# mLSTM with a mixture of experts: gate values computed two steps earlier, list products a position later, VectorE's order within a step changed, six weight loads at later steps

## The chip, the core and the metric

The kernel runs on one core of one Trainium2 chip. The metric is the device time of one execution in microseconds (us); a lower time is better. TensorE (PE) does the matrix products, VectorE (DVE), ScalarE (ACT) and GpSimd (POOL) the elementwise work, SyncE (SP) issues nearly all transfers. Each engine takes its instructions strictly in the order in which the program issues them.

## What is computed

Two parts follow each other: an mLSTM over 4 batches, 8 heads, 768 time steps and head size 40, and a mixture of 8 experts in which each of the 3,072 tokens goes to its best expert alone.

```python
for t in range(S):                                   # mLSTM, state C and n per batch and head
    m_new = max(f_gate[t] + m, i_gate[t])
    f_stab, i_stab = exp(f_gate[t] + m - m_new), exp(i_gate[t] - m_new)
    C = f_stab * C + i_stab * outer(v[t], k[t]);  n = f_stab * n + i_stab * k[t];  m = m_new
    y[t] = sigmoid(o_gate[t]) * (C @ q[t]) / max(|n . q[t]|, 1)
x = y as rows (3072, 320)
logits = normed(x) @ normed(expert_emb).T / tau
e = argmax(logits);  gate = softmax(logits)[e]
out = gate * relu(x @ w1[e]) @ w2[e]
```

## The kernel before, in words

The sequence is cut into 6 chunks of 128 time steps. Chunk times batch gives 24 steps (`NS`), and the loop `for n in range(NS)` (line 1199) writes out the order of every engine's work by hand; there is no planner. Step n handles chunk n // 4 of batch n % 4. The chunk is worked on in two halves of 64.

In one step of the loop, as the program issues it before the change: SP gets the loads of step n+5 (`load_dims`, `load_rows`) and the o-gates of step n+3 (`stage_sig`); PE does `stage_add(n, 0)` (the first half's outer products, added to a state that stays in PSUM, `pcv(n)`); ACT copies that state to `c_mid` (`stage_mid`); VectorE does `stage_next` (line 630) for an earlier step: it writes half of the decayed state to `c_st`, decays the state in PSUM, and ACT later copies the other half (line 1273). PE then does `stage_scores(n + 1)` into the one PSUM tile `s`; POOL does `stage_uv(n + 2)` (values times gate); VectorE does `stage_den(n - 1)` and `stage_x(n - 1)` (the division), POOL `stage_gate(n - 1)`; VectorE does `stage_weigh(n + 1)`, which masks the scores from `s` into `w_s`; PE transposes x of step n-2 (`stage_xt`), does `stage_y(n)`, `stage_add(n, 1)` and the router's logits of step n-3 (`stage_logits`).

Between these steps stands the making of the routing lists: for a group of tokens (`GROUPS`: steps 0 to 5, 6 to 12, 13 to 23) small VectorE operations find the expert (`route_a`), the rank (`route_b`), a one-hot matrix for each step (`route_o`, line 894, into `op`) and an index factor (`route_c`, into `oa`), and PE forms products of them (`route_rank`, `route_ids`, line 899). Which step does what is the table `ROUTE` (line 951). Operations wait in the list `vq`; each `tick()` issues one of them to VectorE, and ticks stand in between the operations of a step. `route(n, 0)` empties `vq` and issues the step's products after `stage_y(n)`; `route(n, 1)` fills `vq` for the next step.

Before the loop the gates of chunk 0 are computed (`gates_scan(0)` and what follows it, lines 1053 to 1075). Those of chunks 1 to 5 go through a chain that crosses four engines: `gates_scan(1)`, `gates_chain` (a scan over the chunks, step 0), `gates_floor` (step 1), `gates_exp` (ACT, step 2), `gates_turn` (products on PE, copies `u_t` and `e_t`, `g_t`, end of step 2), and `stage_uv(4)`, the first to use them. The embeddings of the experts are normed and transposed by `embeddings(0..2)`, at steps 1, 2, 2. Chunks after the first need the gates.

Weight loads of the first two experts (`w_loads`) are issued by SP at the end of the steps that `W_AT` names; at the steps in `W1_AT` ACT and POOL split a loaded piece into two parts. After the loop come the experts: first the two largest with the tokens gathered by `gather_a` (POOL, line 311, at step 21), then the others; this part is left as it is but for `route_o`.

## Time and profile before

| what | value |
|---|---|
| median of 3 runs | 331.6 us (329.17 to 333.5) |
| the profiled execution | 328.59 us |
| its span, first to last instruction | 326.8 us, 1.8 us lie around it |
| mean granted TensorE clock | 0.973 |
| busy: PE, DVE, ACT, POOL | 93%, 69%, 49%, 52% of the span |
| loop, first `stage_y` of step 0 to that of step 23 | 11.66 to 114.20 us |

The table's last line is read from the timeline of PE. Busy shares are means over the loop and the experts, which have different limits; what the change touches lies in the first 115 us. A step is measured here from the first product of its `stage_y` to that of the next.

### The profile page before, as it was taken

The numbers are of one execution on the slowest core, as the hardware profiler recorded it, in microseconds if no ns is written. First come the engines' busy times: TensorE is split into PE (matmuls) and PEld (weight loads), VectorE is DVE, ScalarE is ACT, GpSimd is POOL, SyncE is SP. The second block draws the span as 40 slices with busy tenths as digits, with TensorE's granted clock in tenths as the row PEclk, the third lists the DMA queues.
The fourth block names the chain that finished last, engine by engine and source line by source line (L and its number), as shares of the span: only waits on it lengthen the run. The fifth ranks groups of instructions, "written<-read, shape, count | busy, mean of one in ns | idle before, by whom it ended". The sixth has DMA issues, their size and how long they took to land.

```text
span 326.8 us, 9615 instructions
## 1 busy us (share of the span) xinstructions
PE 302.7 (93%) x3637; PEld 285.8 (87%) x3637; DVE 224.3 (69%) x638; ACT 161.8 (49%) x410; POOL 168.3 (52%) x204
## 2 busy tenths in 40 slices
PE   7877998989997899999969979999999999999992
PEld 3867897978986699989969969999999999999992
DVE  6775777798999479983644786757657586695620
ACT  6394554655564466452332745437427458075310
POOL 8765584757886849350563760650560550832112
PEclk9595999999999799999999999999999999999999
DMA  5896688899999654030277978958837939656001
GB/s 154 301 308 197 185 244 270 254 273 276 256 293 262 225 146 123 3 73 22 70 251 215 304 238 158 301 196 219 262 96 207 321 128 304 196 141 194 20 21 38
DMA packets 48089, 63.31 MB, mean 194 GB/s; under 512 B 21146, under 2 KB 37990, under 8 KB 48034
## 3 DMA queue, kind: packets, MB, share of 16 engines
q1 hardware_dynamic: 45218, 54.16, 56.4%
q0 software_dynamic: 2560, 8.35, 8.4%
q8 instruction: 31, 0.51, 0.7%
q14 instruction: 24, 0.20, 0.2%
q10 hardware_dynamic: 256, 0.10, 0.1%
HBM read 47.51 MB, written 11.93 MB: 182 GB/s over the span
## 4 chain that ended last, share of the span: by engine, by line
PE 76%; DVE 10%; DMA 5%; issue 3%; ACT 3%; POOL 1%; POOLq 0%; SPq 0%; DVEq 0%
PE ph L376 28%; PE po L408 17%; PE s L573 5%; PE po_b L408 4%; PE y L654 4%; PE po_a L408 3%; PE c L612 3%; PE po L393 3%; DMA kv_s<-in_kv 3%; PE y L665 3%; PE pm L731 2%; DMA sig<-in_og 2%; DVE op L896 1%; PE px L717 1%; DVE w_s L582 1%
## 5 line engine op out<-in xcount | busy, mean ns | idle before, releaser
L427 POOL DMA_INDIRECT out<-ob,ids x20 | 22.9, 1145 | 79.2 <-DVE ob L424 70.6
L378 ACT ACTIVATE hh<-ph 128x448 fp32r<-128x448 f32 (+2 forms) x48 | 23.6, 491 | 50.7 <-PE ph L376 36.6
L408 PE MATMUL po<-w2h,hl 128*128 128x320 f32 x128 | 39.6, 309 | 0.0
L408 PE MATMUL po<-w2h,hh 128*128 128x320 f32 x128 | 39.5, 309 | 0.0
L408 PE MATMUL po<-w2l,hh 128*128 128x320 f32 x128 | 39.5, 309 | 0.0
L558 POOL TENSOR_TENSOR uv<-kv_s,u_t 64x328 f32<-64x328 f32 x47 | 34.8, 740 | 8.9 <-PE c L612 4.5
L376 PE MATMUL ph<-xh,w1h 128*128 128x448 f32 (+2 forms) x96 | 32.2, 338 | 1.7 <-DVE hh L383 1.7
L381 DVE SCALAR_TENSOR_TENSOR hl<-ph,hh 128x384 fp32r<-128x384 f32 (+1 forms) x48 | 24.4, 509 | 12.5 <-ACT hh L378 11.7
L376 PE MATMUL ph<-xh,w1l 128*128 128x448 f32 (+2 forms) x96 | 32.0, 336 | 0.0
L573 PE MATMUL s<-kq_s 128*64 128x64 f32 x768 | 29.6, 232 | 1.8 <-DVE w_s L582 1.2
L573 PEld LDWEIGHTS s<-kq_s 128*64 128x64 f32 x768 | 27.4, 146 | 2.9 <-DVE w_s L582 2.2
L197 ACT CAST w1h<-raw 128x512 fp32r<-128x512 f32 x48 | 28.9, 612 | 0.0
L200 DVE TENSOR_TENSOR w2l<-raw,w2h 128x320 fp32r<-128x320 f32 x58 | 28.1, 531 | 0.6
L424 DVE TENSOR_SCALAR ob<-po,gt 128x320 f32<-128x320 f32 x16 | 8.8, 551 | 28.0 <-PE po L408 20.1
L701 POOL TENSOR_TENSOR x<-x,sig 128x320 f32<-128x320 f32 x21 | 18.2, 866 | 17.6 <-DVE x L697 6.9
L612 PE MATMUL c<-uv,kv_s 128*40 128x82 f32 x352 | 24.1, 250 | 2.6 <-issue 1.5
L197 ACT CAST w2h<-raw 128x320 fp32r<-128x320 f32 x62 | 24.4, 457 | 3.2 <-DMA raw<-in_w 2.9
L654 PE MATMUL y<-uv,w_s 128*64 128x82 f32 x384 | 25.7, 250 | 0.0
L628 ACT COPY c_mid<-c 40x164 f32<-40x164 f32 x48 | 14.0, 292 | 23.2 <-PE c L612 22.7
L299 POOL DMA_INDIRECT xs<-x_d,ids x20 | 21.9, 1095 | 6.2 <-issue 5.8
L200 DVE TENSOR_TENSOR w1l<-raw,w1h 128x512 fp32r<-128x512 f32 x36 | 25.1, 706 | 0.0
L376 PE MATMUL ph<-xl,w1h 128*128 128x448 f32 (+2 forms) x96 | 24.5, 336 | 0.0
(314 smaller groups left out, 927.9 us busy)
## 6 DMA issues: line engine op xcount, KB each, us to landing
raw<-in_w SPq DMA_DIRECT2D x32, 320.0 KB
kv_s<-in_kv SPq DMA_DIRECT2D x24, 324.0 KB
kq_s<-in_kq SPq DMA_DIRECT2D x48, 160.0 KB
raw<-in_w SPq DMA_DIRECT2D x14, 512.0 KB
raw<-in_w SPq DMA_DIRECT2D x18, 256.0 KB
sig<-in_og SPq DMA_DIRECT2D x24, 160.0 KB
x_d<-x SPq DMA_DIRECT2D x24, 160.0 KB
x_d<-halves SPq DMA_DIRECT2D x4, 576.0 KB
```

The lines of the kernel that those rows point to most:

```text
L197: A.copy(h, src)
L200: (eng or V).tensor_tensor(lo, src, h.bitcast(F32), ALU.subtract)
L299: G.indirect_dma_start(out=xs[0 : c.shape[0], a], out_offset=None, in_=x_d[0:rows], in_offset=bass.IndirectOffsetOnAxis(ap=c, axis=0), bou ...
L376: T.matmul(ph, lt, rh, start=i == 0, stop=i == len(ops) - 1)
L378: A.activation(hh, ph, AF.Relu)
L381: V.scalar_tensor_tensor(hl[:, 0:m], ph[:, 0:m], 0.0, hh[:, 0:m].bitcast(F32), ALU.max, ALU.subtract)
L408: T.matmul(po[0 : ts_.stop - ts_.start, 0:DM], lt[f][:, ts_], rh[:, f], start=k == 0, stop=k == len(ops) - 1)
L427: store = G.indirect_dma_start(out=out, out_offset=bass.IndirectOffsetOnAxis(ap=slots, axis=0), in_=ob, in_offset=None, bounds_check=NT - ...
L558: eng.tensor_tensor(uv[n % NB][rows, :, :, r], list(rows_of(n))[1][rows], u_t[rows, j, b].unsqueeze(3).broadcast_to([L, 2, NP, D1]), ALU.mult,
L573: T.matmul(s[r * L : r * L + L, c, p], k_of(n, odd)[:, a, cs], q_of(n)[:, a, cs], start=True, stop=True,)
L612: T.matmul(pc[odd * L : odd * L + D, 2 * g : 2 * g + 2], k_rows[:, c, p], uv[n % NB][:, c, p], start=False, stop=g == 1, skip_group_check= ...
L654: T.matmul(yh[c][:, g, :, odd], w_s[n % NB][:, c, 2 * g + odd], uv[n % NB][:, c, 2 * g + odd], start=g + odd == 0, stop=n < B and c == 0, ...
```

## The change

Start: `gates_scan(1)` moves ahead of the first values (it stood after the first `stage_weigh`); `gates_chain` is cut in two (`gates_ends`, `gates_chain`) and both move from step 0 to before the loop; `gates_floor` goes from step 1 to 0; the exponentials from step 2 to 1; a new `gates_spread` (the matrix `gr`, formerly the end of `gates_exp`) stands at step 1; `gates_turn` stays in step 2 but moves ahead of `stage_y(2)`. `c_st` is cleared before the loop, the number tables are made at steps 3 and 5, the embeddings at steps 2, 3, 4, and the two sigmoids and the two warm activations of steps 0 to 2 are put in another order.

Loop: `stage_next` becomes one VectorE operation and stands after `stage_weigh(n + 1)`; both copies to `c_st` go to ACT (`stage_keep`), one step later. `stage_den`, `stage_x`, `stage_weigh`, `stage_next` now follow each other with no ticks between; then come, at one place, the rest of `vq`, the step's products, the new list and nine ticks. The product so stands ahead of `stage_xt` and `stage_y`. `ROUTE` is adapted, `route_o` makes two steps' matrices with one `tensor_tensor` in place of one with each `tensor_scalar`. `W_AT` moves loads to later steps.

```diff
-W_AT = (9, 9, 10, 12, 13, 15, 16, 17, 18, 19, 20, 22)
+W_AT = (9, 10, 12, 14, 16, 18, 19, 20, 21, 22, 22, 23)
-EMB_AT = (1, 2, 2)
+EMB_AT = (2, 3, 4)
...
                 g = g_t[:, j + 1, b].unsqueeze(2).broadcast_to([P, NP, D1])
-                (rows0, dst0, src0), (rows1, dst1, src1) = state_rows(n, c_st[b])
-                V.tensor_tensor(dst1, src1, g[rows1], ALU.mult)
-                tick()
                 V.tensor_tensor(pcv(n), pcv(n), g, ALU.mult)
-                st[n]["next"] = dst0, src0
-                tick()
+
+        def stage_keep(n):
+            if n < NS - B:
+                for rows, dst, src in state_rows(n, c_st[n % B]):
+                    A.copy(dst, src)
...
-            V.tensor_scalar(op, iota_b, grp[g]["lo"][:, b : b + 1], None, ALU.is_equal)
+            V.tensor_tensor(
+                op, iota_b.unsqueeze(1).broadcast_to([P, k, P]), bc(grp[g]["lo"][:, b : b + k], P), ALU.is_equal
+            )
...
-            12: ([], [(place_first,)]),
-            13: ([], [(place_sum,), (route_c, 0)]),
+            12: ([], [(place_first,), (place_sum,)]),
+            13: ([], [(route_c, 0)]),
             14: ([lambda: route_ids(0)], [(route_d, 0)]),
-            15: ([], [(route_a, 1)]),
-            16: ([lambda: route_rank(1)], [(route_b, 1), (gates_early[0],)]),
-            17: ([], [(route_sum, 1), (route_os, 1, 0, 3)]),
-            18: ([early_count], [(route_os, 1, 3, 6), (early_base,), (gates_early[1],)]),
-            19: ([], [(route_os, 1, 6), (route_c, 1)]),
+            16: ([], [(route_a, 1), (gates_early[0],)]),
+            17: ([lambda: route_rank(1)], [(route_b, 1), (route_sum, 1)]),
+            18: ([early_count], [(route_os, 1), (early_base,)]),
+            19: ([], [(gates_early[1],), (route_c, 1)]),
             20: ([lambda: route_ids(1)], [(route_d, 1), (early_ids,)]),
...
         V.tensor_copy(u_t[:, 0]...)
+        gates_scan(1)
         stage_uv(0, (V, G))
         V.tensor_copy(e_t[:, 0]...)
+        for t in c_st:
+            G.memset(t, 0.0)
         stage_uv(1)
-        stage_weigh(0)
-        gates_scan(1)
...
+        gates_ends()
+        stage_weigh(0)
+        gates_chain()
         for n in range(NS):
...
             stage_mid(n)
+            for k in of(n - 1, 1, NEXT_AT):
+                stage_keep(k)
             if n == 1:
-                A.activation(maxc.bitcast(F32), half, AF.Exp)
+                gates_exp()
+                A.activation(maxc.bitcast(F32), half, AF.Sigmoid)
             if n == 2:
-                gates_exp()
-            for k in of(n, 1, NEXT_AT):
-                stage_next(k)
+                stage_sigmoid(1)
             if not last:
                 stage_scores(n + 1)
...
             if n:
-                (stage_den(n - 1, 0..2), stage_x, stage_gate with ticks between)
+                (the same without ticks)
             if not last:
                 stage_weigh(n + 1)
-                tick(2)
+            for k in of(n, 1, NEXT_AT):
+                stage_next(k)
+            route(n)
+            tick(9)
             if n == 0:
-                gates_chain()
-                for t in c_st:
-                    G.memset(t, 0.0)
+                gates_floor()
             if n == 1:
-                gates_floor()
-                numbers()
+                gates_spread()
             if n == 2:
-                more_numbers()
+                gates_turn()
+                stage_uv(n + 2)
+            if n == EMB_AT[2]:
+                embeddings(2)
...
             stage_y(n)
             if n < NS - B:
                 stage_add(n, 1)
-            if n == 2:
-                gates_turn()
-                stage_uv(n + 2)
-            for k in of(n, 0):
-                stage_sigmoid(k)
-            (ACT copies of half of c_st)
+            if n != 1:
+                stage_sigmoid(n)
+            if n == 0:
+                A.activation(maxc.bitcast(F32), half, AF.Exp)
...
-            if not last:
-                route(n, 0)
-            for k in of(n, 3):
+            for k in of(n, 3, (EMB_AT[2],)):
                 stage_logits(k)
-            route(n, 1)
```

## Rows read from the trace of the kernel before

**Rows 1.** Stretches: length; PE, PEld, DVE, ACT, POOL busy us; PEclk, DMA share, GB/s
```profile
11.66:42.44 30.78, 27.07 (x535) 24.73 (x532) 21.73 (x75) 17.68 (x49) 19.81 (x39) 0.83 0.76 246
...
19.48:29.87 10.39, 7.07 (x106) 5.92 (x106) 7.45 (x28) 6.85 (x20) 6.80 (x15) 0.79 0.89 291
29.87:34.67 4.80, 4.80 (x88) 4.56 (x87) 1.30 (x4) 2.07 (x7) 1.62 (x3) 0.73 0.34 97
34.67:38.27 3.60, 3.60 (x96) 3.36 (x95) 2.26 (x8) 2.25 (x8) 2.16 (x3) 1.00 0.67 207
42.44:62.46 20.02, 18.98 (x485) 17.33 (x484) 15.40 (x64) 10.35 (x35) 13.91 (x19) 1.00 0.84 250
62.46:82.82 20.36, 18.88 (x483) 17.21 (x482) 17.19 (x53) 11.88 (x38) 13.92 (x17) 1.00 0.94 282
82.82:107.58 24.76, 22.93 (x571) 20.70 (x570) 23.11 (x76) 14.37 (x46) 19.09 (x23) 1.00 0.96 270
107.58:114.20 6.62, 5.25 (x62) 4.21 (x61) 2.19 (x7) 2.74 (x9) 5.55 (x6) 0.75 0.67 208
```

**Rows 2.** Waits of PE up to 116 us: us in total, times, longest
```profile
PE pen L1188 <- DVE en L1182: 2.5, 1, 2.5
PE pm L903 <- DVE oa L879: 1.8, 2, 1.6
PE c L612 <- issue: 1.5, 2, 1.0
PE s L573 <- DVE w_s L582: 1.2, 2, 0.7
```

**Rows 3.** Chain that ended last, 18 to 28 us: start, us, what
```profile
20.27 1.28 ACT L1116
22.11 0.76 PE pg L1135 x16
25.62 0.54 DVE en L1182
```

**Rows 4.** Timeline of VectorE, start of the kernel: start, us, what, idle before
```profile
8.24 0.49 DVE L558 TENSOR_TENSOR uv<-kv_s,u_t 64x328 f32<-64x328 f32 x1 [1.32 <-DMA kv_s<-in_kv]
9.36 0.41 DVE L1042 TENSOR_TENSOR_SCAN gs<-gf,onef 96x128 f32<-96x128 f32 x1
...
10.12 0.42 DVE L1044 TENSOR_TENSOR_SCAN gp<-gi 96x128 f32<-96x128 f32 x1
...
13.54 1.50 DVE L1091 TENSOR_TENSOR mj<-mm 32x2 f32<-32x2 f32 x3
...
19.41 0.60 DVE L1113 TENSOR_SCALAR gp<-gp,na,cl 96x128 f32<-96x128 f32 x2
```

**Rows 5.** Timeline of ScalarE and of GpSimd, start of the kernel
```profile
15.28 0.60 ACT L628 COPY c_mid<-c 40x164 f32<-40x164 f32 x2 [3.76 <-PE c L612]
...
10.69 1.52 POOL L558 TENSOR_TENSOR uv<-kv_s,u_t 64x328 f32<-64x328 f32 x2 [1.36 <-DMA kv_s<-in_kv]
...
15.08 1.30 POOL L1250 MEMSET c_st<- 128x328 f32 x4
```

**Rows 6.** VectorE's groups, 42.5 to 104.2 us: busy, mean ns, idle before
```profile
L582 DVE TENSOR_TENSOR w_s<-s,late 128x512 f32<-128x512 f32 x15 | 10.2, 681 | 0.0
L697 DVE TENSOR_TENSOR x<-y,den 128x320 f32<-128x320 f32 x15 | 7.4, 491 | 0.7
L636 DVE TENSOR_TENSOR c_st<-c,g_t 40x164 f32<-40x164 f32 x14 | 4.6, 332 | 6.9 <-PE c L612 6.7
```

**Rows 7.** All of the one-hot operations by line: duration ns min/median/max, first and last start
```profile
L896 DVE TENSOR_SCALAR op<-iota_b,lo x24: 242/249/1251, 65.9 to 139.5; 128x128 f16<-128x128 bf16 x24
```

**Rows 8.** Timeline of VectorE and PE around step 20
```profile
95.87 0.68 DVE L582 TENSOR_TENSOR w_s<-s,late 128x512 f32<-128x512 f32 x1
...
101.47 0.33 PE L903 MATMUL pm<-oa,op 128*128 128x32 f16 x7 [1.61 <-DVE oa L879]
```

**Rows 9.** GpSimd's largest group, 42.44 to 104.27 us: busy, mean ns
```profile
L558 POOL TENSOR_TENSOR uv<-kv_s,u_t 64x328 f32<-64x328 f32 x31 | 22.8, 734 | 3.0 <-PE c L612 1.8
```

More of the change, by code (lines that the diff above doesn't have):

```diff
@@ L719, in stage_xt @@
             T.transpose(px[:, 2 * P : 3 * P], x[:, DM - P : DM], ident)
[L720 removed]
+            xt = st[n]["xt"] = tp.tile([P, 3, P], F32, name=f"xt_{n}", tag="xt", bufs=3)
             A.copy(xt.rearrange("p c t -> p (c t)"), px[:, 0 : 3 * P])
@@ L892, in route_sum, with route_o @@
             yield
-        def route_o(g, b):
-            op = sm(g, f"op{b}", [P, P], F16)
-            V.tensor_scalar(op, iota_b, grp[g]["lo"][:, b : b + 1], None, ALU.is_equal)
+        def route_o(g, b, k):
+            op = sm(g, f"op{b}", [P, k, P], F16)
+            grp[g].update({f"op{b + i}": op[:, i] for i in range(k)})
+            V.tensor_tensor(
+                op, iota_b.unsqueeze(1).broadcast_to([P, k, P]), bc(grp[g]["lo"][:, b : b + k], P), ALU.is_equal
+            )
             yield
@@ L911, in route_os @@
         def route_os(g, b0=0, b1=None):
-            for b in range(b0, b1 or nt(g)):
-                yield from route_o(g, b)
+            b1 = b1 or nt(g)
+            for b in range(b0, b1, 2):
+                yield from route_o(g, b, min(2, b1 - b))
         def cntv(g):
@@ L978, in tick, with route @@
                         vq.pop(0)
-        def route(n, i):
-            if i == 0:
-                while vq:
-                    tick()
-                for f in ROUTE.get(n, [[]] * 2)[0]:
-                    f()
-            else:
-                vq.extend(f(*a) for f, *a in ROUTE.get(n, [[]] * 2)[1])
+        def route(n):
+            while vq:
+                tick()
+            products, lists = ROUTE.get(n, ([], []))
+            for f in products:
+                f()
+            vq.extend(f(*a) for f, *a in lists)
         warm = pX.tile([P, 512], F32, name="warm", tag="px")
@@ L1227, in tile_mlstm_moe @@
                 gates_early[2]()
-            if n == NS - 3:
-                while vq:
-                    tick()
             if n:
-                stage_den(n - 1, 0)
-                tick()
-                stage_den(n - 1, 1)
-                tick()
-                stage_den(n - 1, 2)
+                for k in range(3):
+                    stage_den(n - 1, k)
                 stage_x(n - 1)
@@ L1265, in tile_mlstm_moe @@
                 stage_add(n, 1)
-            if n == 2:
-                gates_turn()
-                stage_uv(n + 2)
-            for k in of(n, 0):
-                stage_sigmoid(k)
-            for k in of(n, 1, NEXT_AT):
-                if "next" in st[k]:
-                    A.copy(*st[k]["next"])
+            if n != 1:
+                stage_sigmoid(n)
+            if n == 0:
+                A.activation(maxc.bitcast(F32), half, AF.Exp)
             for k in of(n, 1):
@@ L1277, in tile_mlstm_moe @@
                 stage_sq(k)
-            for k in range(3):
-                if EMB_AT[k] == n:
-                    embeddings(k)
-            if not last:
-                route(n, 0)
-            for k in of(n, 3):
+            if n in EMB_AT[:2]:
+                embeddings(EMB_AT.index(n))
+            if n == 3:
+                numbers()
+            if n in (5, 6):
+                G.memset(xs_a[:, n - 5], 0.0)
+            if n == 5:
+                more_numbers()
+            for k in of(n, 3, (EMB_AT[2],)):
                 stage_logits(k)
-            route(n, 1)
             for _ in range(W_AT.count(n)):
```

23 lines of the change are left out of this document (12 added, 11 removed).

## The prediction

> **What bounds the kernel now.** I read the busy time by stretches first, cut at the first product of each `stage_y`, then PE's waits, then the chain in the stretch that is longest, and last the timelines of the engines that the chain names. The plain step 4 takes 3.60 us with PE busy for all of it at the full clock, VectorE for 2.26 and GpSimd for 2.16 [rows 1]. So PE's own work sets the step, and whatever a step takes over 3.60 is what a change of order can win. The sums over the loop: steps 0 to 5 take 30.78 us where six plain steps take 21.6; steps 6 to 10 take 20.02 against 18.0; steps 11 to 15 20.36 against 18.0; steps 16 to 21 24.76 against about 21.0 (21.6 less two times 0.3, since steps 20 and 21 have no `stage_add(n, 1)`; an estimate: eight of some 96 products); step 22 6.62, with two extra turns of gathered rows and PE's clock at 0.75 [rows 1]. PE's waits name the causes: 2.5 us for the embeddings' norm, 1.8 for `oa`, 1.2 for the masked scores, 1.5 for nothing that the profile shows [rows 2].
>
> Most of the surplus is step 2, with 10.39 us, and step 3, with 4.80 us at a mean clock of 0.73, that is in part at 1.2 GHz, since PE had idled before it [rows 1]. The chain there is the gate chain that the change moves: the exponentials begin with a table load of 1.28 us on ScalarE at 20.27, the turn on PE starts at 22.11, then VectorE scales the embeddings at 25.62, and only behind their transposes PE takes up step 3 [rows 3].
>
> **The start, part by part.** `gates_scan(1)` is three operations from 9.36 to 10.54, 1.2 us. Ahead of `stage_uv(0)` VectorE idles 1.32 us for a transfer [rows 4]; the scan fills that, cost nothing; without that cover it would put the first values back by 1.2. The clearing of `c_st`, 1.30 us on GpSimd, goes into its wait of 1.36 us ahead of `stage_uv(1)` [rows 5], cost nothing, at worst 1.3. The rest of `gates_chain` starts behind the first mask, some 2.5 us earlier than now; its three small copies to `mj` took 1.50 us [rows 4], next to a GpSimd operation, and will meet another one, `stage_uv(1)`. `gates_floor` now ends at 20.01 [rows 4]; one step earlier, with the chain earlier too, I put it at 15.5. Behind it on VectorE stand den, x and the mask of step 2, late by some 0.4 us, which PE does not see: the mask is wanted only by the next scores. On ScalarE the exp table is now loaded in an idle stretch of 3.76 us before 15.28 [rows 5], so that the exponentials follow `stage_mid(1)` at 15.9 and end at about 17; the table for the sigmoid follows them, 1.28 us, and `stage_mid(2)` is through at about 19.1. PE has the turn to do right after `stage_scores(3)`, some half us ahead of the 19.48 at which step 2 begins now, and nothing that it needs is late by then. It costs PE what it costs now, 1.5 us (22.11 to where the chain leaves PE), but it is now in the way of `stage_y(2)`, where formerly PE idled behind it. Behind the turn ScalarE copies `u_t`, and GpSimd does `stage_uv(4)` until about 22.5; PE wants it two steps on, at about 26. The embeddings' three transposes, about 0.4 us, come at step 4 when the norm of step 3 is long done. So step 2 becomes 3.6 + 1.5, step 3 has no idle before it and runs at the full clock, and in step 5 nothing waits for the copies of `c_st`, which now come a step later and well before `stage_y(n + 4)`.
>
> Steps 0 to 5 then: 21.6, plus 0.65 for step 0 at the half clock as now (an estimate: its excess is unchanged), 1.5 for the turn, 0.4 for the transposes: 24.1 instead of 30.78 [rows 1]. **Gain 6.7 us.** Bounds: 3.5, if the chain is late by a whole step after all; 7.5, if the turn is hidden in part.
>
> SP issues the same loads in nearly the same order (o-gates of step 1 one load earlier, the embeddings one earlier); each queue keeps its work. The number tables move to steps 3 and 5 of GpSimd, which is busy for 2.16 of 3.60 us [rows 1], so 1.4 a step are free for them.
>
> **The lists.** VectorE loses one operation of 332 ns in each of 14 steps [rows 6], 4.6 us over the loop; ScalarE gets a second copy of about that length and was busy 2.25 of 3.60 us [rows 1], so that costs nothing. VectorE's fixed work in a step becomes 2.26 - 0.33 = 1.9 us, and 1.7 are left for lists. Its idle ahead of line 636, 6.7 us for `stage_add` of PE [rows 6], goes, as den and x need only `stage_y`. The mask now stands ahead of the list work; so what is queued behind a long list is den and x of the next step and then its mask, and PE meets it only if the list runs over by more than about 1.7 us (an estimate: 3.60, less the 1.2 that the 32 scores take as a third of a step's 96 products, less the mask's 0.68).
>
> Steps 11 to 15 have 17.19 us of VectorE's work in 20.36; five of the removed operations take 1.6 out [rows 1, 6], and lists of up to 2.5 us follow plain ones, so the surplus should go but for the product of `route_ids(0)`, 0.3. **Gain 2.0 us** (0.8 to 2.2). Steps 6 to 10: 2.02 us of surplus, of which 1.04 is a single wait of PE for nothing shown [rows 2] that I can't tie to any of it, and 0.4 products that stay: gain 0.2 (0 to 1.3).
>
> Steps 16 to 21 are the hard part. VectorE is busy 23.11 of 24.76 us [rows 1]. Removed are four times 0.33. The one-hot operations of group 1 fall from seven to four, but each does 256 columns where one took 242 ns undisturbed for 128 [rows 7]; no row shows the new form, and between 0.24 and 0.48 for two I take 0.4, so this is even. And `route_ids(1)` moves forward on PE, ahead of `stage_y(20)`, while its last input stays in the list of step 19: now it comes 4.9 us after the mask of 95.87 (which ended at 96.55), and PE waited 1.61 for it at the end of a step [rows 8]. In the new order that list has nine operations in one piece, about 4 us; the mask's 0.68, the decay's 0.33 and the list add to about 5.0 from the end of the scores, and PE is back at the product after 3.6: a wait of 1.4 if VectorE is on time, up to 3.4 if it runs two us late. I take 2.3. So surplus 3.76 falls to 0.6 of products and 2.3: **gain 0.8 us** (-0.6 to 2.3).
>
> **The weight loads.** The queue's share is 0.94 to 0.96 through steps 11 to 21 and 0.67 in step 22 [rows 1], so a later load finds room, and the pieces of the first matrix still come two or three steps after their load. The second matrix and the second expert's are split only behind the loop, and the last of them is issued where now the last but one is. No gain, no loss; if one is late, the split of it blocks ScalarE and with it the relu of the experts. Step 22 keeps its 6.62 us: GpSimd's gathers and PE's unexplained waits there are not touched (0 to 2.5 gain). After the loop only the one-hot operations of group 2 change, eleven to six: 0 (-0.5 to 0.5).
>
> **Sum.** 6.7 + 0.2 + 2.0 + 0.8 = 9.7 us off the profiled execution's 328.6: 318.9. The median of the runs lies 3.0 above that execution, outside its 1.8 us around the span, and the runs scatter by 4.3; taken from the median the sum gives 321.9. I put the time between, **320.5 us**.
>
> **A rule that speaks against it.** A list operation of 242 ns took up to 1,251 [rows 7], and `mj` 1.50 us for three tiny ones [rows 4]. The Trainium skill, SBUF — State Buffer, Who interferes with whom, says that a VectorE operation with two SBUF inputs, or in a two-port mode, and a GpSimd operation that reads SBUF shut each other out for their whole length, while one that reads PSUM goes by its own port. By that rule den, x and the mask don't wait but the lists do, and lists in one piece wait at every operation of GpSimd; the trace agrees in that the mask's mean is 681 ns and x's 491 without such outliers [rows 6]. What it would make of the time is rival four.
>
> **Rivals.** One (0.15): the wait for `oa` grows instead of shrinking, and the late lists reach the scores. For it: VectorE has only 1.65 us of idle in steps 16 to 21 [rows 1]. A wait of 5 us at step 20 in place of 2.3 and 0.5 of scores: 3.2 more, 323.7. Two (0.13): transfers become the bound once PE is faster, or the gate chain of the start still ends a step late. For it: the queue's share of 0.94 to 0.96 at 270 to 282 GB/s [rows 1]. Against: PE hardly waited for a transfer. Steps 0 to 5 carried 30.78 x 246 = 7.6 MB; in 24.1 us that is 314 GB/s, but the loads run five steps ahead. If the gain of the start is 3.5 in place of 6.7, or later steps lose as much, about 325. Three (0.10): PE's waits for nothing shown, 1.5 us [rows 2], and the half clock of step 22 go too: 3.5 less, 317. Four, the other side (0.05): the lists in one piece wait for GpSimd. About 45 of their operations read SBUF alone (my count of the table's lists); each waiting for a whole `stage_uv` half of 734 ns [rows 9] makes 33 us, some 10 of which are paid now (the 24 one-hot operations alone have a minimum of 242 and a maximum of 1,251 [rows 7]). 23 more on steps 6 to 21, where VectorE has 65.14 - 55.7 + 5 = 14 us free [rows 1, 6], is 9 over: then the loop from there is 9 us longer than now and not 3 shorter, 320.5 + 12 = 332.5; with GpSimd's longer operations up to 340. It turns the sign from about 20 us of added waits on.
>
> **Chances.** The forecast has 0.57, with a range of its own of 316.5 to 324. The measurement can tell 2% from no change, that is 6.6 us, so faster means under 325. Of the forecast nine tenths (0.51), of one six tenths (0.09), of two 0.02 and of three all (0.10) lie there: 0.72. Slower is the worse half of four, 0.03. The rest is 0.25. The range of 315 to 326.5 leaves out the best of three, the worst of two and four.
>
> **What would show it.** Right: the first `stage_y` of step 6 at about 35.5 in place of 42.44; no half clock between 20 and 35 us; four table loads in ScalarE's first 30 us; steps 11 to 15 under 18.7; a wait of PE for `oa` at step 20 of 1.4 to 3.4. Wrong: if step 2 is still over 6 us, some link of the chain (the exponentials behind `stage_mid(1)`, or `gr`) was late; if PE waits for `w_s` or a transfer in steps 6 to 19; if the experts' part, now 212 us of the span behind 114.20, grows.

## The result: half of the forecast gain, and the profile after

The changed kernel took 325.26 us (median of 4 runs, 323.04 to 326.53), the kernel before 332.52 beside it; the ratio is 0.987, interval 0.982 to 0.992 (ratios leave disturbed executions out, so they need not be the quotient of the two medians). The forecast was 320.5 us. The profiled execution took 324.12 us with a span of 322.3, where the one before took 328.59: 4.5 us less, of the 9.7 that the sum had. The first `stage_y` of step 0 comes at 12.28 us (before: 11.66), that of step 23 at 109.92 (114.20). The time by stretches, each between the first products of `stage_y`:

| stretch | before | after | forecast | measured |
|---|---|---|---|---|
| to `stage_y(0)` | 11.66 | 12.28 | 0 | +0.6 |
| steps 0 to 5 | 30.78 | 21.91 | -6.7 | -8.9 |
| steps 6 to 10 | 20.02 | 21.07 | -0.2 | +1.0 |
| steps 11 to 15 | 20.36 | 18.13 | -2.0 | -2.2 |
| steps 16 to 21 | 24.76 | 32.30 | -0.8 | +7.5 |
| step 22 | 6.62 | 4.23 | 0 | -2.4 |
| step 23 and the experts | 212.6 | 212.4 | 0 | -0.2 |

The busy time of the changed kernel by stretches, with the columns of [rows 1]:

```profile
12.28:34.19 21.91, 21.86 (x534) 20.30 (x531) 16.53 (x59) 16.36 (x52) 18.41 (x36) 0.99 0.91 292
34.19:55.26 21.07, 18.64 (x484) 17.22 (x484) 18.02 (x64) 12.90 (x42) 14.93 (x19) 1.00 0.88 274
55.26:73.39 18.13, 18.13 (x482) 16.95 (x481) 11.79 (x37) 13.90 (x43) 13.37 (x16) 1.00 0.93 270
73.39:105.69 32.30, 25.34 (x572) 22.79 (x571) 25.15 (x72) 16.13 (x51) 24.62 (x28) 0.93 0.82 242
93.92:98.81 4.89, 4.89 (x88) 4.66 (x87) 3.40 (x12) 2.47 (x8) 3.57 (x5) 0.65 0.66 154
98.81:105.69 6.88, 4.89 (x89) 3.88 (x88) 3.66 (x7) 2.39 (x7) 5.95 (x6) 0.94 0.58 165
105.69:109.92 4.23, 4.23 (x62) 3.95 (x61) 1.76 (x6) 2.26 (x8) 0.54 (x1) 0.70 0.73 235
```

In the first and third row PE is busy for all but 0.05 us: nothing is left to win there by taking waits away. In steps 16 to 21 PE's busy time rose from 22.93 to 25.34 us for the same products, mostly because the clock's mean fell from 1.00 to 0.93, and PE idles for the other 6.96 us, where it idled 1.83 before [rows 1]. Step 20 (fifth row) has no wait in it and still takes 4.89 us at a mean clock of 0.65, that is mostly at 1.2 GHz. The timeline of PE in the changed kernel gives the waits, each in front of the line in whose brackets it stands (`issue` marks a wait for nothing that the profile shows):

```profile
55.00 0.33 PE L718 MATMUL px<-ident,x 128*128 128x128 f32 x1 [2.43 <-issue]
...
78.06 0.30 PE L716 MATMUL px<-ident,x 128*128 128x128 f32 x1 [1.16 <-ACT xt L720]
87.13 0.69 PE L571 MATMUL s<-kq_s 128*64 128x64 f32 x17 [1.82 <-issue]
93.28 0.33 PE L905 MATMUL pm<-oa,op 128*128 128x32 f16 x7 [1.87 <-DVE oa L878]
101.41 0.38 PE L571 MATMUL s<-kq_s 128*64 128x64 f32 x5 [0.39 <-issue]
...
104.42 0.50 PE L571 MATMUL s<-kq_s 128*64 128x64 f32 x9 [0.37 <-issue]
```

The last two are the first and the fifth of a row of five, 1.98 us together. So of the 8.3 us by which steps 16 to 21 missed the forecast's 24.0, about 1.3 are the copy of the transposed rows at step 16 (`act_late` below measures it), 1.8 are the wait for nothing shown at 87.13, 1.6 the low clock in step 20 (4.89 against 3.3 us at the full clock) and 3.6 step 21 (6.88 against the 3.3 us that the same step takes in other runs); the wait for `oa`, 1.87, is 0.4 shorter than forecast. That is 7.9 of 8.3. Steps 21 and 22 belong together: before the change a row of three such short waits stood in step 22, at 109.0 to 110.9 us, and now one stands in step 21. The two steps take 11.11 us together, 9.93 before, so of the 3.6 us some 2.4 come back in step 22.

ScalarE's timeline in the changed kernel shows where the wait at step 16 comes from:

```profile
76.80 0.29 ACT L453 ACTIVATE sn<-lg_all 128x104 f32<-128x104 f32 x1 [3.47 <-DVE lg_all L451]
77.12 0.29 ACT L454 ACTIVATE lg_all<-lg_all 128x104 f32<-128x104 f32 x1
77.43 0.48 ACT L720 COPY xt<-px 128x384 f32<-128x384 f32 x1
```

The list of step 16 ends in two activations of the early gates. With the list now issued ahead of `stage_xt`, they stand ahead of its copy on ScalarE, which idles 3.47 us for VectorE's list and lets PE wait for `xt`. The prediction costed the activations nowhere.

### The profile page after: what moved, and what is told of

It reads as the page before. It is cut to its first block, busy times and chain, and to the rows that moved or that the text cites. A ratio compares the mean times of both kernels' runs of the same rounds, so it can differ in the third digit from the quotient of the medians.

```text
span 322.3 us, 9598 instructions
## 1 busy us (share of the span) xinstructions
PE 299.6 (93%) x3637; PEld 284.5 (88%) x3637; DVE 217.6 (68%) x607; ACT 167.2 (52%) x429; POOL 169.6 (53%) x205
## 4 chain that ended last, share of the span: by engine, by line
PE 77%; DVE 11%; ACT 4%; issue 3%; DMA 3%; another core or an unknown queue 0%; POOL 0%; POOLq 0%; DVEq 0%; ACTq 0%; SPq 0%
PE ph L374 27%; PE po L406 17%; PE s L571 7%; PE y L653 4%; PE po_b L406 4%; PE y L664 3%; PE c L610 3%; PE po L391 3%; DMA kq_s<-in_kq 2%; PE pm L730 2%; PE po_a L406 2%; PE px L716 1%; ACT w2h L195 1%; DMA x_d<-x 1%; DVE w_s L580 1%
## 5 line engine op out<-in xcount | busy, mean ns | idle before, releaser
L425 POOL DMA_INDIRECT out<-ob,ids x20 | 22.2, 1112 | 75.4 <-DVE ob L422 64.6
L571 PE MATMUL s<-kq_s 128*64 128x64 f32 x768 | 30.5, 230 | 4.6 <-issue 3.8
L422 DVE TENSOR_SCALAR ob<-po,gt 128x320 f32<-128x320 f32 x16 | 8.8, 550 | 27.9 <-PE po L406 19.8
L198 DVE TENSOR_TENSOR w2l<-raw,w2h 128x320 fp32r<-128x320 f32 x58 | 26.5, 504 | 1.1 <-ACT w2h L195 0.5
L297 POOL DMA_INDIRECT xs<-x_d,ids x20 | 22.9, 1143 | 6.2 <-issue 5.8
L653 PE MATMUL y<-uv,w_s 128*64 128x82 f32 x384 | 24.8, 249 | 0.0
L626 ACT COPY c_mid<-c 40x164 f32<-40x164 f32 x48 | 14.0, 292 | 19.7 <-PE c L610 15.6
L406 PEld LDWEIGHTS po<-w2l,hh 128*128 128x128 f32 x128 | 24.0, 188 | 0.0
L406 PEld LDWEIGHTS po<-w2h,hh 128*128 128x128 f32 x128 | 24.0, 188 | 0.0
```

The costliest lines, as they stand in the source:

```text
L198: (eng or V).tensor_tensor(lo, src, h.bitcast(F32), ALU.subtract)
L297: G.indirect_dma_start(out=xs[0 : c.shape[0], a], out_offset=None, in_=x_d[0:rows], in_offset=bass.IndirectOffsetOnAxis(ap=c, axis=0), bou ...
L406: T.matmul(po[0 : ts_.stop - ts_.start, 0:DM], lt[f][:, ts_], rh[:, f], start=k == 0, stop=k == len(ops) - 1)
L425: store = G.indirect_dma_start(out=out, out_offset=bass.IndirectOffsetOnAxis(ap=slots, axis=0), in_=ob, in_offset=None, bounds_check=NT - ...
L571: T.matmul(s[r * L : r * L + L, c, p], k_of(n, odd)[:, a, cs], q_of(n)[:, a, cs], start=True, stop=True,)
L626: A.copy(dst, src)
```

## The experiments

They ran in five sets, on four chips that are called A to D here, each set beside the kernel before on the same chip. The median of the kernel before was 326.08 and 326.55 us in the two sets on chip A, 329.93 on B, 331.47 on C and 326.48 on D. Which chip gave the result above (332.52) isn't on record. All other medians are compared within their set only; the set on B has no unedited changed kernel.

**The changed kernel again**, four times, nothing edited.

> The changed kernel once more, as the base for the others. Theory A (the instructions of PE come late when the transfers are dense, so its waits for nothing shown are not tied to a place): about 325 us as before, but the long waits of 2.43 us at step 10 and 1.82 us at step 18 fall in other steps or have other lengths. Theory B (these waits belong to fixed places of the program): the same waits at the same steps within 0.3 us. Under both the wait for oa at step 20 stays at about 1.9 us and that for the copy of xt at step 16 at about 1.2 us.

> The changed kernel once more, beside the three that follow. Both theories: ratio 0.971 to 0.987, the wait for nothing shown at 55 us of 2.0 to 2.8 us, steps 6 to 10 about 21 us, a wait of 1.2 us for the copy of the transposed rows at step 16, one of 1.9 to 2.5 us for the index factor at step 20.

> The changed kernel once more, as the base of this call. If the chip is one with waits of 0.4 us at 100 to 105 us: ratio about 0.985, steps 16 to 21 about 32 us with a wait of 1.8 to 2.0 us at 87 us. If it is one without: ratio 0.972, steps 16 to 21 28 to 29 us.

> The changed kernel once more, as the base. On a chip where transfers are slower: the store of the early gates leaves SyncE 2 to 5 us after its data are there, the first gather starts at 98.5 to 102 us, PE waits for gathered rows at step 22 or shows 0.4 us waits in step 21, ratio 0.985. On a chip like the second: the store leaves within 0.5 us, ratio 0.972.

| set | changed | before | ratio |
|---|---|---|---|
| first on A (`after_again`) | 318.15 | 326.08 | 0.971 (0.966 to 0.976) |
| second on A (`after_third`) | 318.67 | 326.55 | 0.973 (0.960 to 0.986) |
| C (`after_fourth`) | 328.82 | 331.47 | 0.986 (0.973 to 0.999) |
| D (`after_fifth`) | 318.02 | 326.48 | 0.973 (0.968 to 0.978) |

Where the kernel before is at 326 us the change wins 2.8%, near the forecast; on C, where it is at 331, it wins 1.4%, and its four times scatter from 323.7 to 330.4. The profile on C shows none of the waits of 0.4 us, and yet the ratio is not 0.972: neither branch of that expectation held.

The waits for nothing shown are at the same two products as above but not of the same length (2.01, 2.56, 1.73 and 2.28 us at step 10; 0.45, 0.36, none and 0.63 at step 18), which is half of each theory of `after_again`. The step tables of the profiles on A and D differ from the one above. Steps 6 to 10 take 20.7 to 21.7 us, steps 11 to 15 19.7 to 19.8 in place of 18.13, steps 16 to 21 29.2, 27.9 and 26.3 in place of 32.30, and steps 21 and 22 together 6.4, 6.4 and 8.4 in place of 11.1. The clock makes most of the difference in steps 11 to 15: in these three the half clock followed the wait at step 10 and step 11 took 5.2 us, in the profile above it did not, and step 11 took 3.60. Step 20 is the other way round on D, where a wait of 2.21 us for `oa` was followed by the full clock. Both in one view each, step 11 of `after_again` and step 20 of `after_fifth`:

```profile
55.15:60.35 5.20, 5.20 (x97) 4.96 (x96) 1.38 (x5) 2.98 (x9) 3.06 (x4) 0.67 0.88 281
```

```profile
95.22:98.53 3.31, 3.31 (x88) 3.07 (x87) 3.08 (x12) 2.47 (x8) 2.30 (x3) 1.00 0.40 81
```

**The start alone** (`start_only` on A, `start_again` on C): the kernel before with all edits ahead of and in steps 0 to 5, and before's lists, `stage_next` and weight loads.

> The kernel before with the changes of the start alone (gates, tables, embeddings, the sigmoids of steps 0 to 2); VectorE's order, the lists, the one-hot operations and the weight loads as before. Theory A: step 6 begins at about 34.5 us as in the changed kernel, steps 11 to 21 take 45 us as before, in all 6.5 to 8 us less than before, that is as much as the whole change or more. Theory B (the lists were worth their 2 us and the loss is of the start's making, by denser transfers): 3 to 4 us less than before, with steps 16 to 21 longer than 27 us.

> The kernel before with the start of the change alone. Theory A (the lists' part pays for itself in step 22 and little else): ratio to the kernel before 0.980 to 0.985, 1.5 to 2 us over the changed kernel of the same call on either chip. Theory B (on a chip with the gathers' waits the lists' part is worth nothing): within 0.7 us of the changed kernel there.

Measured 320.28 us, ratio 0.983 (0.978 to 0.987), and on C 322.83, ratio 0.974 (0.963 to 0.984), beside 0.971 and 0.986 for the whole change. So the start carries most of the gain: steps 0 to 5 take 23.4 and 22.8 us there. The other part (lists, VectorE's order, loads) added 1.2% on A, and on C the whole change was 1.2% above the start alone, with intervals that overlap: no gain from it is shown there. On A neither theory held as worded (5.8 us less than before, steps 16 to 21 in 26.0), on C neither (6 us under the changed kernel).

**Two waits taken away** (`act_late`, `c_first`, then `both`).

```diff
 root():                          # act_late
-  A.activation(sn, ...); A.activation(lg, ...)
+  (issued at step 16 behind stage_sq)
-19: ([], [(gates_early[1],), (route_c, 1)]),   # c_first
+19: ([], [(route_c, 1), (gates_early[1],)]),
```

> The two sigmoid activations that the list of step 16 issues on ScalarE ahead of the copy of xt stand at the end of step 16 instead; all else as in the changed kernel. Theory A: ScalarE's idle of 3.5 us ahead of them and PE's wait of 1.16 us for the copy of xt go, steps 16 and 17 take 7.5 to 7.9 us instead of 9.2, 1.0 to 1.5 us less in all. Theory B (VectorE bound): the same time is lost two steps later, 0.3 us less or nothing.

> In the list of step 19 the index factor (route_c) stands ahead of the six gate operations; all else as in the changed kernel. Theory A (the loss of steps 16 to 21 is made of single waits, one of which is oa, and of the half clock behind it): PE's wait for oa at step 20 of 1.87 us goes, so does the half clock that follows it, 2.5 to 3 us less than the changed kernel. Theory B (VectorE's total in these steps is the bound, and a wait taken away comes back at the next place): less than 0.7 us less.

> The changed kernel with two edits together: the index factor ahead of the early output gates in the list of step 19, and the two activations of the early gates issued on ScalarE behind the copy of the transposed rows at step 16. Alone each took its wait away and moved no time. Theory A: VectorE is full in steps 16 to 21, so the wait comes again further on (for the state's decay at step 20), steps 16 to 21 take 26.5 to 28 us, and the ratio is 0.968 to 0.973, no better than the changed kernel. Theory B: the two waits were added to each other by the late start of VectorE, and without both the steps take under 25.5 us, ratio 0.962.

Measured 318.32 us (0.973, 0.966 to 0.980), 318.55 (0.977, 0.970 to 0.984) and, on B, 322.95 (0.983, 0.974 to 0.993). The first edit does what it says: step 16 takes 3.80 us in place of 5.11, with PE busy for all of it, in the row of `act_late` for this step:

```profile
75.83:79.63 3.80, 3.80 (x105) 3.56 (x104) 3.53 (x13) 1.67 (x6) 3.65 (x5) 1.00 0.97 280
```

And yet the time is that of the changed kernel. With `c_first` PE's timeline shows why:

```profile
91.42 0.33 PE L905 MATMUL pm<-oa,op 128*128 128x32 f16 x7 [0.66 <-DVE oa L878]
96.01 0.77 PE L610 MATMUL c<-uv,kv_s 128*40 128x82 f32 x8 [2.29 <-DVE c L633]
```

The wait for `oa` falls to 0.66 us, and a wait of 2.29 for the next thing that VectorE owes, the decay of the state, takes its place. VectorE is the bound of steps 18 to 20, so the order of its list chooses which product waits, and hardly how long PE waits in all. With both edits the wait for VectorE falls to 0.48, but two waits for nothing shown, 1.90 and 0.48 us, stand in steps 18 and 20, in which VectorE catches up. The sums bear this out: PE's waits in steps 18 to 20 add to 2.94, 2.94 and 2.84 us in the unedited kernel on A and D, to 3.00 in `act_late`, 2.92 in `heavy` and 2.86 in `both`, whether PE waits for `oa`, for the decay or for nothing shown (3.31 in `c_first`, 3.69 in the first profile of the changed kernel).

**VectorE's list shortened** (`no_share`): the six operations of `gates_early[1]` left out, the early gates set to 1 instead.

> The changed kernel without the six VectorE operations of the second part of the early output gates, which stand ahead of the index factor in the list of step 19 (the gates of the gathered tokens are set to 1 instead, so this part of the result is left out). Theory A: VectorE's list work sets steps 18 to 21: some 1.5 us less of it shortens PE's wait for the index factor from 1.9 to 2.5 us to under 1.2, steps 16 to 21 fall from 29 (28.2 to 29.2 on the second chip) to 27 to 27.5, no half clock follows, and the ratio to the kernel before is about 0.966. Theory B: PE's clock and its waits for nothing shown set those steps: the wait moves on, steps 16 to 21 stay at 28 to 29, and the ratio stays at 0.971.

Measured 321.69 us, ratio 0.976 (0.967 to 0.986) and not the 0.966 of theory A. The wait for `oa` is gone; PE's timeline has the products of line 905 without one:

```profile
88.77 0.93 PE L571 MATMUL s<-kq_s 128*64 128x64 f32 x17 [2.01 <-issue]
94.51 0.34 PE L905 MATMUL pm<-oa,op 128*128 128x32 f16 x7
```

That the lists cause the wait for `oa` is shown: the wait of 2.01 us is all that PE waits in steps 18 to 20, where 2.8 to 3.0 is the rule. Steps 16 to 21 take 27.9 us, of which the wait at 88.77 is 2.0, and the half clock follows it: with some 1.5 us less of VectorE's work they still don't come near 24.

**The waits for nothing shown.** `light` leaves out the o-gates' loads from chunk 2 on, 16 of 24, 160 KB each (chunks 2 to 5 use those of chunks 0 and 1). `late_w` moves the first weight loads to steps 11 to 13. `heavy` adds a load of 80 KB in each of 16 steps.

```diff
+if j > 1: sigs[j] = sigs[j - 2]; return                   # light
-W_AT = (9, 10, 12, 14, ...  W1_AT = (11, 13, 15, 17,      # late_w
+W_AT = (11, 12, 13, 14, ... W1_AT = (13, 15, 16, 17,
+if 3 <= n < 19: SY.dma_start(spare, og[:, n, 0 : DM // 2])  # heavy
```

> The changed kernel without 16 of its 24 loads of o-gates (160 KB each, from chunk 2 on; chunks 2 to 5 multiply by the gates of chunks 0 and 1 instead, so this part of the result is left out). Theory A: PE's waits for nothing shown at about 55 us (2.0 to 2.4 us) and 87 us (0.4 to 1.8 us) come from an instruction transfer that is late because the DMA engines are full; with some 16% less to carry the wait at 55 us falls under 0.5 us, steps 6 to 10 take 18.5 to 19.5 us in place of 21.0, and the ratio to the kernel before is 0.960 to 0.966. Theory B: the wait belongs to its place in the program, whatever the transfers do: it stays at 2.0 to 2.4 us at the same product, steps 6 to 10 stay at about 21, and the ratio stays at 0.971.

> The changed kernel with the first loads of weights at steps 11 to 13 instead of 9 to 12, and their pieces split two or three steps later. Theory A: PE's wait at 55 us is an instruction transfer that is late behind the first two weight loads, which are issued at about 51 us on top of a full queue: without them there it falls under 0.7 us, steps 6 to 10 take about 19 us, and steps 11 to 15 stay under 19.5; some 2 us less than the changed kernel of the same call, ratio to it about 0.994. Theory B: the loads of the steps fill the queue by themselves; the wait stays at 2 us or over, steps 6 to 10 at 21 us, and the time stays within 1 us of the changed kernel's.

> The changed kernel with one more load of 80 KB, that nothing reads, in each of the steps 3 to 18 (1.3 MB in all, about 8% more of what the loop carries). Theory A (instruction transfers come late because the DMA engines are full): PE's waits for nothing shown in steps 6 to 20 grow from 2.4 to 4.2 us in sum to 6 us and over, in more places than two, and the time rises by 3 to 6 us. Theory B (the place in the program decides): the same one or two waits of the same length, time within 1.5 us of the changed kernel's unless loads of the steps themselves come late, which would show as waits of PE for a transfer.

Of `light` the loop alone can be read, since its altered rows change what the experts have to do (6,037 us there). Its steps 6 to 10:

```profile
34.87:53.58 18.71, 18.59 (x485) 17.07 (x484) 16.28 (x59) 12.90 (x42) 14.54 (x19) 1.00 0.86 272
```

18.71 us in place of 21.07 (21.5, 21.4 and 19.4 in `both`, `no_share` and `old_loads`, on the same chip as `light`), and no wait over 0.12 us at that product or at step 18. Theory A of `light` came true for these waits. What differs is when one instruction transfer starts (queue 8). In the changed kernel none starts from 45.2 to 52.2 us; then, between 52.2 and 53.1 us, its DMA queues have this row (packets, MB, share):

```profile
q8 instruction: 1, 0.02, 8.4%
```

and the same row of `light` between 50.6 and 51.0 us:

```profile
q8 instruction: 1, 0.02, 17.0%
```

The late one starts at 52.32 us, 2.7 us before PE's wait ends; that of `light` at 50.71, and there is no wait. In all profiles the waits of 0.9 us and more for nothing shown end 2.4 to 2.8 us after the start of such a transfer.

Their places follow from a count. In the changed kernel's traces 2,242 of PE's instructions (products and weight loads) stand ahead of the one that waits at step 10, and 3,777 ahead of the one at step 18; in `best` the wait of 1.08 us has 1,986 ahead of it, in the kernel before that of 1.04 has 1,729. All differences are multiples of 256 to within one record. A transfer has 16,384 bytes, and queue 8 starts one for each 256 instructions of PE, so a transfer carries 256 of them. PE takes some 5 us for so many, and in the changed kernel the late transfer starts 4.80 us after PE passed the boundary before (47.52 us), in `light` 2.51 us after it. The rows of 0.4 us waits are not at such boundaries; they are something else.

But the amount of traffic doesn't set the delay by itself. `late_w` (320.61 us, 0.983, 0.972 to 0.993) has 0.91 us of this wait with no weight load near it, between its two theories, and is not faster; with the two other edits added (`best`, below) the waits are 2.28 and another 1.08. `heavy` (328.87 us, 0.992, 0.986 to 0.997) carries more and has 1.21 us of it, less than the 2.56 of `plain_gather_2` beside it, which has no such loads. So theory A of `heavy` fell as far as these waits go, and theory B with it, as the wait's length is not fixed either. The time of `heavy` can't be told from that of the changed kernel on the same chip (328.82, 0.986); the 3 to 6 us of theory A aren't seen. The product at step 10 is the same in all kernels with the whole change, the length is 0 to 2.8 us. Where the wait stands is thus shown, and that it ends with a late transfer; what makes the transfer late stays open.

`heavy` has waits elsewhere: a piece of a weight stands ahead of the copy of the state on ScalarE, and waits for its load,

```profile
58.72 0.62 ACT L195 CAST w1h<-raw 128x512 fp32r<-128x512 f32 x1 [3.77 <-DMA raw<-in_w]
59.24 0.59 ACT L626 COPY c_mid<-c 40x164 f32<-40x164 f32 x2
```

after which PE waits 2.11 us for `c_mid`. The prediction had named this block of ScalarE by a late piece, but for the experts; and the gathers come late, which is the next point.

**The gathers.** `plain_gather` (again as `plain_gather_2`) loads fixed rows in place of the four gathers of the first two experts, so those tokens' outputs are left out.

```diff
-gather_rows(xs_a[:, e, a : a + 1], [ids_a[:, e, a : a + 1]], ...)
+SY.dma_start(xs_a[:, e, a, 0:DM], x_d[i * P : (i + 1) * P, 0:DM])
```

> The changed kernel with the four gathers of the first two experts' tokens replaced by plain loads of fixed rows by SyncE (the right tokens and their gates are left out, so the outputs of these tokens are not computed). Theory A: PE's row of waits of 0.4 us for nothing shown at 100 to 105 us comes from the gathers that GpSimd issues then: without them there are none, step 21 takes 3.3 to 3.7 us whatever the chip. Theory B: they come from an instruction transfer at about 101 us that is late on its own account: they stay at 1.5 to 2 us in sum where the changed kernel of the same call shows them.

> The four gathers replaced by plain loads of fixed rows by SyncE (the right tokens and their gates are left out). On a chip where the changed kernel shows the row of 0.4 us waits at 100 to 105 us: theory A (the gathers cause them) none are left, steps 21 and 22 take 6.5 us together in place of 9 to 11, and the time falls by 2 to 4 us; theory B (a late instruction transfer) they stay at 1.5 to 2 us in sum and the time stays within 1 us. On a chip without them: no difference, as 318.03 to 318.67 us before.

On A: 318.03 us, ratio 0.975 (0.967 to 0.982), beside 318.67 for the unedited kernel. On C: 320.86, ratio 0.969 (0.959 to 0.978), beside 328.82 and 0.986 (0.973 to 0.999); the intervals just overlap. So on C the gathers, with what they wait for, cost by the medians about what the change fell short by; with this overlap it is likely and not shown. Step 22 of `plain_gather_2`, where `heavy` on the same chip takes 9.41 us and `start_again` 7.30:

```profile
103.99:107.03 3.04, 3.04 (x62) 2.76 (x61) 2.33 (x7) 2.26 (x8) 1.17 (x1) 1.00 0.69 213
```

The timeline of `heavy` shows the chain that ends in the gathers:

```profile
92.65 0.37 DVE L468 COPY sw<-se 128x208 f32<-128x208 f32 x1
97.14 1.27 SPq L472 DMA_DIRECT2D x_d<-sw  x1
102.66 1.30 POOL L297 DMA_INDIRECT xs_a<-x_d,ids_a  x1 [3.23 <-DMA x_d<-sw]
```

The early gates are in `sw` at about 93.0 us. Their store stands on SP behind the loads and row stores of steps 19 and 20 and is issued 4.1 us later; it takes 5.5 more until it lets GpSimd go, and PE then waits 3.17 us for the first and 1.90 for a later gathered tile. In `start_again` the store is issued 2.4 us after `sw` is ready and PE waits 3.24. The changed kernel's five waits of 0.4 us at 101 to 105 us are another matter: no profile on C or A shows them, so neither `plain_gather` could test them. `light`, `both` and `no_share`, all on B, and the kernel before have such rows of three or four waits. In these five profiles the row begins 2.5 to 3.3 us after the first gather, but thirteen other profiles have the same four gathers and no row. Whether they come from the gathers stays open.

**The store out of SP's queue** (`put_act`): ScalarE issues it.

```diff
-SY.dma_start(x_d[n0 * P : n1 * P, DM:XW], sw)
+(SY if n0 else A).dma_start(x_d[n0 * P : n1 * P, DM:XW], sw)
```

> The changed kernel with the one store of the early gates (104 KB in rows of 64 bytes) issued by ScalarE in place of SyncE, so that it doesn't stand behind the loads and row stores of steps 19 and 20. Theory A (that queue holds the gathers back): the store leaves within 1.5 us of its data, the first gather starts some 2 us or more earlier in step 20 or 21, PE's waits for gathered rows are gone, and where the base shows these waits the time falls by 3 to 6 us; on a chip where the base has none it stays within 1 us. Theory B (the store is late in landing because the DMA engines are full, whichever queue it is in): the first gather starts as late as before and the time stays within 1 us.

Measured 317.50 us beside 318.02, both 0.973. This was on D, on which the unedited kernel issues the store 0.02 us after `sw` is ready, and in both kernels the first gather starts behind GpSimd's own work, not behind the store; so it tells nothing of the other chips. The edit is open there.

**Loads and the three edits together** (`old_loads`: before's `W_AT`; `best`: `act_late`, `c_first` and `late_w`).

> The changed kernel with the weight loads at the steps of the kernel before. Theory A: the place of the loads costs nothing and gains nothing: ratio 0.968 to 0.975, steps 6 to 10 and 16 to 21 within 1 us of the changed kernel's. Theory B: the denser loads of steps 9 to 17 make the late instruction transfers later: the wait at 55 us grows to 3 us and more and steps 11 to 15 take over 20.5 us, ratio 0.978; what steps 18 to 22 gain by fewer loads is under 1 us.

> The three edits together: index factor ahead of the early output gates, the two activations of the early gates behind the copy of the transposed rows, first weight loads from step 11 on. Theory A: the waits at 55 us, at step 16 and at step 20 all go; steps 6 to 10 take about 19, steps 16 to 21 24.5 to 26 us; some 5 us less than the changed kernel of the same call. Theory B: what is won at the first two comes back as waits for VectorE at steps 20 and 21 and for the gathered rows at step 22: at most 2 us less.

`old_loads` took 326.26 us, 0.989 (0.981 to 0.998), on B, beside `both` with 322.95 and `no_share` with 321.69: neither theory. Its wait at step 10 is 0.95 us, not longer, but steps 11 to 15 take 20.39 and step 22 takes 8.62, with 4.57 us for gathered rows. The store of the early gates is issued at 95.31, 3 us after its data, with the first gather at 101.36. That hints that moving the six loads was worth something after all, by a path that the prediction didn't see; it isn't shown, as the unedited changed kernel wasn't run on B. `best` took 320.15 us, 0.983 (0.973 to 0.993), 318.67 being the changed kernel's: theory B. It won 1.3 us at step 16 and has waits of 2.29 for VectorE's decay, 1.03 for `oa`, and 2.28 and 1.08 for nothing shown. No version with the whole result is shown to beat the changed kernel.

## Why the prediction was half right

**The start: right in mechanism, gain larger than its upper bound.** Step 6 begins at 34.19 us (forecast 35.5; 34.1 to 35.1 in the profiles on A and D). The timelines of the changed kernel, VectorE and then PE, have the floor's last operation done by 15.4 us (forecast 15.5) and the turn at 18.04 to 19.52, 1.48 us (forecast 1.5):

```profile
14.27 1.10 DVE L1119 TENSOR_SCALAR gp<-gp,na,cl 96x128 f32<-96x128 f32 x2
```

```profile
18.04 0.69 PE L1143 MATMUL pg<-ident,gu 96*64 96x48 f32 x16
...
19.34 0.18 PE L1163 MATMUL pg<-flag,ones 96*128 96x2 bf16 x1
```

The four table loads and the full clock between 20 and 35 us came as forecast. The turn falls into step 1 (4.88 us), and step 2 takes 3.27, since it has fewer products than the 96 of a plain step: the sum had 3.6 for each step, 21.6 in all, which was too much for steps 0, 2 and 3 (74, 76 and 80 products). `stage_y(0)` comes 0.6 us later here, which was costed at nothing; but in the profiles of kernels with this start it comes anywhere from 11.17 to 12.64 us, so this is not shown to be a price of the change.

**Steps 11 to 15: right on VectorE, lucky on the clock**, 18.13 (forecast under 18.7). VectorE holds up no product there any more, as forecast; but in the profiles on A and D these steps take 19.7 and more, as the half clock behind the wait at step 10 falls into step 11, and the sum has no term for that.

**The one-hot operations: even**, as forecast: group 1's four take 3.26 us by their durations where seven took 3.32. Both are above what undisturbed ones would take; all of the new form:

```profile
L896 DVE TENSOR_TENSOR op<-iota_b,lo x13: 278/418/1077, 53.4 to 134.9; 128x256 f16<-128x256 bf16 x11, 128x128 f16<-128x128 bf16 x2
```

The median 418 ns is the forecast's 0.4. In step 18 three of them took 0.95 to 1.08 us, next to GpSimd's operations on `uv` and `x`. By the Trainium skill, SBUF — State Buffer, Who interferes with whom, an operation with two SBUF inputs contends with a GpSimd operation that reads SBUF; this trace agrees, with 1.0 against 0.42 us. Rival four, that this would turn the sign, did not come: in this profile PE waits for VectorE from step 0 to 22 only for `oa`, 1.87 us. Its mechanism seems to have come, though, in that very wait: on VectorE's timeline the last three operations ahead of the product, beside GpSimd's `uv`, take 2.26 us, 0.76 in the kernel before:

```profile
90.90 0.62 DVE L872 TENSOR_TENSOR a<-ge 128x28 f16<-128x28 f32 x1
91.56 0.66 DVE L875 TENSOR_TENSOR a<-a,tok 128x28 f16<-128x28 f16 x1
92.25 0.98 DVE L878 TENSOR_TENSOR oa<-oh_all,a 128x224 f16<-128x224 bf16 x1
```

**Steps 16 to 21: the step that failed**, a gain of 0.8 us forecast, a loss of 7.5 measured (a loss of 1.5 to 4.4 against the same 24.76 in the profiles on A and D). The wait for `oa` was right (1.87, and 2.2 to 2.6 in those profiles; forecast 1.4 to 3.4). The sum allowed for 0.6 us of products and one wait of 2.3 and for nothing else. Four things were missing. The clock: rows of step 22 before [rows 1] showed 0.75 behind waits, but the sum let PE go on at 2.4 GHz after a wait of 2 us, while step 20 ran at 0.65, 1.6 us; this came in three of the four profiles on the result's chip, A and D, not in all. The move of the list ahead of `stage_xt`: its price was sought on VectorE and PE alone, and it lay on ScalarE, 1.3 us. PE's waits for nothing shown: they were rival three, as something that might go; instead the one of 1.04 us in [rows 2] went and two came at other products, 2.43 at step 10 and 1.82 at step 18. The first of these made steps 6 to 10 miss too (+1.0 in place of -0.2). And the row of short waits in step 21, 3.6 us with what stands between them: the sum left such waits in step 22, where they were. Its cause stays open.

**Step 22 and the gathers.** "Not touched" was wrong. GpSimd's gathers are reached by a chain (list, store, gather) that the change moves, and in the changed kernel step 22 takes 4.23 us, but step 21 takes 6.88. On chips where the store is late, the gathers seem to give back part of what the loop wins, which is rival two at a place that the prediction didn't name. (Its price there was 3.2 us by the prediction's own terms, 323.7 and not about 325.)

**The choice of the base.** The forecast lay between 318.9 (from the profiled execution) and 321.9 (from the median). On the chips with before at 326 us the changed kernel takes 318, 8 us less, and the sum had 9.7. That it comes near there is luck and not the working: in the first profile on A steps 16 to 21 take 29.2 us where the sum put 24.0, and steps 6 to 15 40.7 where it put 38.2; steps 0 to 5, with 22.5 for 24.1, step 22, with 3.0 for 6.6, and the experts, 2.8 us shorter than in the kernel before on its chip, make up for it. That one and the same edit wins 1.3% on one chip and 2.8% on another was in none of the cases.

## What to carry to other kernels

When a list of one engine moves in the program, cost every instruction that its operations issue on other engines: here two activations at the list's end held up a copy that PE wanted. When an engine is full over several steps, an edit of the order moves the wait to its next debt; here only less work shortened the waits, from 2.8 to 3.0 us to 2.01. And cost a wait of PE by what may follow it too: behind the wait of 1.87 us the clock took another 1.6 us from the next step, while in another execution a wait of 2.21 at the same product was followed by the full clock.

## What the runs showed of the hardware

The same program differs between chips by 1 to 3%, and the effect of a change differs with it: the changed kernel took 318.0 to 318.7 us in three sets of runs and 325.3 and 328.8 in two, the kernel before 326 to 327 and 331 to 333 beside it.

PE can stand for 0.9 to 2.8 us with nothing to wait for but its own instructions: each such wait ends 2.4 to 2.8 us after a transfer of instructions has started, and such waits stand a multiple of 256 of PE's instructions apart, to within one record (behind 1,729, 1,986, 2,242 or 3,777 of them), which is what one transfer of 16,384 bytes carries.

The granted clock falls to half behind some waits of PE of about 2 us and not behind others at the same product: the changed kernel's wait at step 10 was followed by 1.00 after 2.43 us in one profile and by 0.67 in step 11 after 2.01 in another; that for `oa` by 0.65 in step 20 after 1.87 and by 1.00 after 2.21.

A store of 104 KB in rows of 64 bytes kept the gathers behind it waiting for 5.5 us from its issue in `heavy`. By the Trainium skill, DMA: Bandwidth & Descriptors, Issuing engines are not separate DMA queues, another issuing engine saves only the time on the sequencer; in `put_act` the issue came 0.03 us after its data, in the unedited kernel beside it 0.02, so no run here shows whether that holds for the 4.1 us that the store stood on SP.
